# Fewer loaded bytes and an earlier buffer release in a kernel of strided sparse attention and spectral mixing on one core

## The chip, the cores and the metric

The kernel runs on one core of a Trainium2 chip. The metric is the device time of one execution in microseconds. Three executions of the kernel before gave 451.14 us as their median (450.7 to 451.53).

## The reference, cut to what matters

```python
# attention: q, k, v are (8 batches, 8 heads, 576, 64)
scores = q @ k.T / 8
mask   = local (0 <= rel < 32) for heads 0-3, strided (rel >= 0, same residue mod 32) for heads 4-7
x      = softmax(where(mask, scores, -1e9)) @ v            # -> (8, 576, 512)
# spectral mixing: w_r, w_i are (64 modes, 512, 512), w_ch is (512, 512)
X  = rfft(x, axis=1)[:, :64]
Yr = Xr @ w_r - Xi @ w_i          # per mode
Yi = Xr @ w_i + Xi @ w_r
u  = x + irfft(Y, n=576)
out = u + relu(u @ w_ch)
```

Two facts carry the change. The 128 MiB of w_r and w_i in float32 are by far the largest input. And in mode 0 of a real signal Xi is zero and the inverse transform ignores Yi, so w_i of mode 0 is never needed.

## The kernel before

The program has four stages on one instruction order per engine. First the strided heads of 8 batches (to about 99 us). Then the local heads, interleaved with the 64 modes of one half of the channels. Then the 64 modes of the other half, interleaved with transposes of x and products with w_ch. Last a tail that turns spectra into rows and writes the result.

Weights come as float32 and are written as float16 by transfers that GpSimd issues. One mode and half is a tile, filled by two transfers of 256 KB:

```python
for ri, src in enumerate([moe_w_r, moe_w_i]):       # w_fetch
    nc.gpsimd.dma_start(wt[ds(64 * ri, 64)],
        src[m, ds(256 * half, 256), :].rearrange("(p c) e -> p c e", c=4))
```

Twelve buffers and six "guest" places (modes 3 to 6, and 16 and 17, in memory that other data needs later) hold 18 tiles. `mode(slot, m)` does a mode's 16 matmuls and then asks for one more tile, unless its own tile was a guest:

```python
if slot or m not in GUEST:
    w_fetch()
```

In the second stage each batch does 8 modes, spread over 19 pieces of attention work, so mode 7 is the very last thing of batch 0:

```python
for mi in range(8):
    upto = -(-len(work) * (mi + 1) // 8)
    for w in work[n:upto]: w()
    n = upto
    mode(0, 8 * b + mi)
```

The strided stage loads q, k and v of a batch as 72 rows of 2048, three tiles deep:

```python
nc.gpsimd.dma_start(qn[0:72, vi, :],
    src[i, 4:8].rearrange("h (c r) d -> (h c) (r d)", r=32))
```

w_ch is loaded twice, once in plain order and once (`w_cp`, four transfers) in the order in which x lies. The masks are constants already repeated for three or four heads.

The softmax here doesn't subtract the row's maximum and nothing guards it: scores larger than these inputs give would overflow.

Of the kernel before, what the change touches and what calls it, by code (L numbers as in the profile page):

```python
# [11 lines left out]
F16 = mybir.dt.float16  # L12
# [6 lines left out]
DM = 512  # L19
# [10 lines left out]
def _host_consts():  # L30
    s = np.arange(S)
    m = np.arange(NM)
    ang = 2.0 * np.pi * np.outer(s, m) / S
    F3 = np.stack([np.sin(ang), np.cos(ang), -np.sin(ang)], axis=1)
    F3 = F3.reshape(S, 3 * NM)

    Fl = np.zeros((128, 5, 3 * NM))
    for t in range(5):
        Fl[: SCS[t], t] = F3[128 * t : 128 * t + SCS[t]]
    Fs = np.zeros((128, 6, 3 * NM))  # L40
    for rp in range(2):
        for j, (a, z) in enumerate(JG):
            r2 = np.arange(a, z)
            ss = (32 * np.arange(NCB)[None, :] + 2 * r2[:, None] + rp).reshape(-1)
            Fs[: len(ss), 3 * rp + j] = F3[ss]



    A = np.zeros((4, 2, 16, S))
    for mm in range(NM):  # L50
        e = np.zeros(S // 2 + 1, dtype=np.complex128)
        for ri, unit in enumerate((1.0, 1j)):
            e[mm] = unit
            A[mm // 16, ri, mm % 16] = np.fft.irfft(e, n=S)
    A = A.reshape(2 * NM, S)
    A[:, :512] = A[:, :512].reshape(128, 256, 2).transpose(0, 2, 1).reshape(128, 512)

    ms = []
    for nr in (6, 5):
        n = nr * NCB  # L60
        kc, kr = np.arange(n) // nr, np.arange(n) % nr
        qr, qc = np.arange(n) // NCB, np.arange(n) % NCB
        ok = (kr[:, None] == qr[None, :]) & (kc[:, None] <= qc[None, :])
        blk = np.zeros((128, n))
        blk[:n] = np.where(ok, 0.0, NEG)
        ms.append(np.tile(blk, (1, 4)))

    rel = np.arange(160)[None, :] - np.arange(128)[:, None]
    blk = np.where((rel >= 0) & (rel < STRIDE), 0.0, NEG)
    ma = np.tile(blk, (1, 3))  # L70
    last = np.full((128, 96), NEG)
    last[:64, 32:] = blk[:64, :64]
    mb = np.tile(np.concatenate([blk, last], axis=1), (1, 2))
    f16 = [a.astype(np.float16) for a in (Fl, Fs, A, ms[0], ms[1], ma, mb)]
    return f16 + [np.eye(128, dtype=np.float16)]


# [1 line left out]
def kernel(  # L79
# [31 lines left out]
        return pss[kind].tile([128, 512], FP, tag=kind, name=kind)  # L111

    hosts = _host_consts()
    names = ["cFl", "cFs", "cA", "cM6", "cM5", "cMa", "cMb", "cI"]
    drams = {
        n: nc.inline_tensor(np.ascontiguousarray(h), name=n).ap()
        for n, h in zip(names, hosts)
# [5 lines left out]
    def const_load(eng, *which):  # L123
        for n in which:
            eng.dma_start(cs[n], drams[n])

    idn = cs["cI"]


    XC = [0, 2, 1, 3]  # L130
# [33 lines left out]
    def w_fetch(n=1):  # L164
        for _ in range(n):
            i = len(w_tiles)
            if i >= 2 * NM:
                return
            half, m = 1 - i // NM, i % NM
            if i in GUEST:  # L170
                n, j = GUEST[i]
                if j == 0:
                    guests[n] = big.tile([128, 2, 4, DM], F16, tag=n, name="wt")
                wt = guests[n][:, j]
            else:
                wt = pw.tile([128, 4, DM], F16, tag="w", name="wt")
            for ri, src in enumerate([moe_w_r, moe_w_i]):
                nc.gpsimd.dma_start(  # L178
                    wt[ds(64 * ri, 64)],
                    src[m, ds(256 * half, 256), :].rearrange("(p c) e -> p c e", c=4),  # L180
                )
            w_tiles.append(wt)

    def w_cp_fetch():
        w_cp = pw.tile([128, 4, DM], F16, tag="w", name="w_cp")
        for c2 in range(2):
            for half in range(2):
                nc.gpsimd.dma_start(
                    w_cp[ds(64 * c2, 64), ds(2 * half, 2), :],
                    moe_w_ch[ds(256 * half, 256), :].rearrange(  # L190
                        "(p cp c2) e -> c2 p cp e", cp=2, c2=2
                    )[c2],
                )
        w_chs["cp"] = w_cp


    qns = {}
# [113 lines left out]
    def str_scores(b, t):  # L311
        qT, kz = qTs[b % 2], kzs[b % 2]
        j, rp = STR[t]
        a, z = JG[j]
        n = (z - a) * NCB
        mask = cs["cM6"] if j == 0 else cs["cM5"]
        scp = psum("sc")
        nc.tensor.matmul(scp[:, 0 : 4 * n], idn, mask, start=True, stop=False)
        for h in range(4):
            nc.tensor.matmul(  # L320
                scp[:, ds(n * h, n)],
                kz[:, rp, ds(72 * a + n * h, 128)],
                qT[:, ds(288 * h + a * NCB, n)],
                start=False,
                stop=(h == 3),
            )
        nc.scalar.activation(  # L327
            out=PS[0:n, ds(POFF[t], 4 * n)],
            in_=scp[0:n, 0 : 4 * n],
            func=ACTF.Exp,  # L330
            scale=SCALE,
        )
# [71 lines left out]
    def loc_scores(b, h, tail):  # L404
        par, hp = b % 2, h // 2
        scp = psum("sc")
        nc.tensor.matmul(  # L407
            scp if tail else scp[:, 0:480],
            idn,
            cs["cMb"] if tail else cs["cMa"],  # L410
            start=True,
            stop=False,
        )
        todo = []
        if tail:
            for hh in range(2):
                todo.append((256 * hh, 576 * hh + 384, 160))
                todo.append((256 * hh + 192, 576 * hh + 512, 64))
        else:
            for t in range(3):  # L420
                todo.append((160 * t, 576 * (h % 2) + 128 * t, 160))
        for i, (col, s0, n) in enumerate(todo):
            nc.tensor.matmul(  # L423
                scp[:, ds(col, n)],
                kzs[par][:, hp, ds(s0, 128)],
                qTs[par][:, ds(s0, n)],
                start=False,
                stop=(i == len(todo) - 1),
            )
        PV = PL[:, 0:4096].rearrange("p (h x) -> p h x", h=4)  # L430
        if tail:
            dst = PV[:, ds(2 * hp, 2), 768:1024]
            src = scp.rearrange("p (h x) -> p h x", h=2)
        else:
            dst = PV[:, h, 0:768].rearrange("p (t x) -> p t x", t=3)[:, :, 0:160]
            src = scp[:, 0:480].rearrange("p (t x) -> p t x", t=3)
        nc.scalar.activation(out=dst, in_=src, func=ACTF.Exp, scale=SCALE)  # L437
# [64 lines left out]
    def mode(slot, m):  # L502
        half = 1 - slot
        mi, mg = m % 8, m // 8
        if mi == 0:
            ypt[slot] = psum("y")
        yp = ypt[slot]
        yv = yp.rearrange("p (m e x) -> p m e x", m=8, e=4)
        wt = w_tiles[slot * NM + m]
        for e in range(4):  # L510
            for c in range(4):
                nc.tensor.matmul(  # L512
                    yv[:, mi, e, :],
                    wt[:, XC[c], ds(128 * e, 128)],
                    Xh[half][:, c, :, :, m],
                    start=(c == 0),
                    stop=(c == 3),
                )
        if slot or m not in GUEST:
            w_fetch()  # L520
        if mi == 7:
            part = (slice(None), slice(None), mg // 2, slice(None), ds(8 * (mg % 2), 8))
            src = yp.rearrange("p (m e x) -> p e x m", m=8, e=4)
            if slot == 0:
                if m == 7:
                    spectra_tile("Y0")
                nc.scalar.activation(out=YS["Y0"][part], in_=src, func=ACTF.Copy)
            else:
                nc.vector.tensor_tensor(
                    out=YS["YT"][part], in0=src, in1=YS["Y0"][part], op=AluOp.add  # L530
                )
# [134 lines left out]
    load(0)  # L666
    const_load(nc.scalar, "cI", "cM6", "cM5", "cFs")
    load(1)
    const_load(nc.sync, "cMa", "cMb", "cFl", "cA")
    load(2)  # L670
    w_fetch(2)

# [54 lines left out]


    psum_pools(tp=2, sc=2, av=2, y=2)
    for b in range(B):  # L730
        load(B + b + 3)
        front = loc_front(b + 1)
# [6 lines left out]
            values[2], front[6], values[3], front[7], lambda: dft(b, 0),  # L739
        ]  # L740
        if b == 6:
            work.insert(0, w_cp_fetch)
        n = 0
        for mi in range(8):
            upto = -(-len(work) * (mi + 1) // 8)
            for w in work[n:upto]:
                w()
            n = upto
            mode(0, 8 * b + mi)
    actx.close()  # L750
    spectra_tile("YT")

# [3 lines left out]
    xoh = [ptr.tile([128, DM], F16, name=f"xoh{i}") for i in range(4)]  # L756
    zzs = [ptr.tile([128, DM], F16, name=f"zz{i}") for i in range(B)]
    yys = [ptr.tile([128, DM], F16, name=f"yy{i}") for i in range(B)]
    w_chs["n"] = ptr.tile([128, 4, DM], F16, name="w_ch")
    nc.gpsimd.dma_start(w_chs["n"], moe_w_ch.rearrange("(c p) e -> p c e", p=128))  # L760
    work = []
    for b in range(B):
        for half, cp in ((1, 0), (1, 1), (0, 0), (0, 1)):
            work.append(lambda b=b, half=half, cp=cp: turn(b, half, cp))
# [128 lines left out]
```

## Time and profile before

| what | value | how to read it |
|---|---|---|
| span of the profiled execution | 448.4 us | the profile's own clock; the measured time is about 2 us more |
| share of software DMA queue | 94.1% of 16 engines | weights, q, k, v and w_ch |
| chain that ended last | DMA 52%, TensorE 19% | followed back from the last instruction |
| TensorE busy | 341.4 us (76%) | not the bound |
| last weight landed | 408.37 us | from the semaphore records of the trace |
| tail after it | 40.0 us | 448.4 - 408.4 |

A software transfer here ends with one completion from each of the 16 DMA engines, and the trace has the time of each. The Trainium skill, "DMA: Bandwidth & Descriptors", Why a DMA increments its semaphore by 16 and not by 1, describes it so: all 16 engines post one increment, each behind its own data. The trace agrees: every one of these transfers has 16 completion times. The completion times carry no engine's number: "the last engine" below is the one that came last for that transfer, and need not be the same one each time.

### The profile page before, as it was taken

The numbers are of one execution on the slowest core, as the hardware profiler recorded it, in microseconds if no ns is written. First come the engines' busy times: TensorE is split into PE (matmuls) and PEld (weight loads), VectorE is DVE, ScalarE is ACT, GpSimd is POOL, SyncE is SP. The second block draws the span as 40 slices with busy tenths as digits, with TensorE's granted clock in tenths as the row PEclk, the third lists the DMA queues.
The fourth block names the chain that finished last, engine by engine and source line by source line (L and its number), as shares of the span: only waits on it lengthen the run. The fifth ranks groups of instructions, "written<-read, shape, count | busy, mean of one in ns | idle before, by whom it ended". The sixth has DMA issues, their size and how long they took to land.

```text
span 448.4 us, 12268 instructions
## 1 busy us (share of the span) xinstructions
PE 341.4 (76%) x5269; PEld 242.9 (54%) x5269; DVE 215.0 (48%) x461; ACT 185.8 (41%) x349; POOL 183.1 (41%) x332
## 2 busy tenths in 40 slices
PE   2887687769898986848875585877859687787994
PEld 2766576647676865646654353545536454543441
DVE  3687767846443542323311242336344543542895
ACT  1586666554554552514341120213314221342883
POOL 4233333332544343444444343434344444420773
PEclk9998979899987895756555575768797886888999
DMA  8999999999999999999999999999999999992687
GB/s 200 197 198 200 203 197 203 209 211 208 165 211 210 214 210 212 210 213 212 212 207 208 212 212 211 212 212 211 213 203 212 213 211 212 212 211 48 261 313 272
DMA packets 31637, 93.72 MB, mean 209 GB/s; under 512 B 5792, under 2 KB 7584, under 8 KB 31584
## 3 DMA queue, kind: packets, MB, share of 16 engines
q0 software_dynamic: 27344, 82.33, 94.1%
q1 hardware_dynamic: 3664, 10.09, 6.1%
q8 instruction: 41, 0.67, 0.6%
q10 hardware_dynamic: 576, 0.53, 0.4%
q14 instruction: 12, 0.10, 0.1%
HBM read 165.80 MB, written 9.44 MB: 391 GB/s over the span
## 4 chain that ended last, share of the span: by engine, by line
DMA 52%; PE 19%; issue 3%; ACT 2%; DVE 1%; POOL 0%; DVEq 0%; ACTq 0%; POOLq 0%
DMA wt<-in_moe_w_i_dram 43%; DMA wt<-in_moe_w_r_dram 6%; PE y L512 4%; DMA qn<-in_k_dram 2%; PE tp L362 2%; PE v L803 2%; PE sc L407 2%; PE v L634 1%; PE u L652 1%; PE y L480 1%; PE sc L423 1%; PE u L650 1%; PE av L444 1%; ACT X L233 1%; PE z L621 1%
## 5 line engine op out<-in xcount | busy, mean ns | idle before, releaser
L512 PE MATMUL y<-X,wt 128*128 128x16 f16 x2048 | 83.0, 192 | 67.2 <-DMA wt<-in_moe_w_i_dram 62.1
L178 POOL DMA_DIRECT2D wt<-in_moe_w_r_dram x128 | 66.3, 518 | 122.1 <-DMA wt<-in_moe_w_r_dram 30.4
L512 PEld LDWEIGHTS <-wt 128*128 128x128 f16 x2048 | 72.8, 103 | 79.7 <-issue 71.7
L178 POOL DMA_DIRECT2D wt<-in_moe_w_i_dram x128 | 66.2, 517 | 74.3 <-DMA wt<-in_moe_w_i_dram 41.3
L608 ACT ACTIVATE v<-sc 128x512 f16<-128x512 f32 x32 | 19.1, 597 | 88.2 <-PE sc L599 88.2
L599 PE MATMUL sc<-w_cp,xT 128*128 128x512 f16 (+1 forms) x160 | 52.4, 457 | 0.5 <-DVE xT L571 0.5
L437 ACT ACTIVATE PL<-sc 128x480 f16<-128x480 f32 (+1 forms) x48 | 27.3, 579 | 50.9 <-PE sc L423 49.7
L609 DVE COPY xo<-tp 128x512 f16<-128x512 f16 x32 | 22.1, 692 | 50.7 <-PE tp L607 50.7
L223 DVE TENSOR_TENSOR xb<-av,rec 90x256 f16<-90x256 f32 (+2 forms) x80 | 36.0, 450 | 2.8
L222 DVE RECIPROCAL rec<-av 90x4 f32<-90x4 f32 (+2 forms) x80 | 14.7, 184 | 42.0 <-PE av L452 29.0
L369 DVE COPY qT<-tp 128x576 f16<-128x576 f16 x16 | 12.1, 759 | 40.8 <-PE tp L362 36.7
L233 ACT ACTIVATE v<-tp 128x640 f16<-128x640 f16 (+1 forms) x24 | 19.4, 807 | 23.2 <-PE tp L396 19.7
L362 PE MATMUL tp<-cI_s,qn 64*64 64x64 f16 x864 | 25.9, 210 | 3.4 <-DMA qn<-in_q_dram 2.2
L327 ACT ACTIVATE PS<-sc 90x360 f16<-90x360 f32 (+1 forms) x48 | 22.7, 488 | 11.0 <-PE sc L320 10.5
L827 DVE TENSOR_TENSOR osb<-u,rl 128x512 f32<-128x512 f32 x36 | 23.3, 688 | 6.2 <-ACT rl L812 3.2
L815 POOL TENSOR_TENSOR rl<-rl,xo 128x512 f32<-128x512 f32 x15 | 17.3, 1158 | 20.0 <-ACT rl L812 19.6
L362 PEld LDWEIGHTS <-qn 64*64 64x64 f16 x864 | 20.3, 123 | 9.0 <-issue 3.8
L258 PE MATMUL tp<-cI_s,qn 72*128 72x72 f16 x256 | 15.1, 209 | 12.5 <-DMA qn<-in_v_dram 9.6
L627 ACT ACTIVATE zz<-av 32x512 f16<-32x512 f32 x24 | 14.1, 588 | 24.1 <-PE av L621 23.9
L369 DVE COPY vT<-tp 128x576 f16<-128x576 f16 x16 | 12.1, 758 | 23.5 <-PE tp L362 23.5
L423 PE MATMUL sc<-qT,kz 128*128 128x160 f16 (+1 forms) x160 | 23.0, 272 | 0.0
L599 PEld LDWEIGHTS <-xT 128*128 128x128 f16 (+1 forms) x160 | 14.7, 110 | 15.3 <-issue 7.2
(91 smaller groups left out, 659.3 us busy)
## 6 DMA issues: line engine op xcount, KB each, us to landing
wt<-in_moe_w_r_dram POOLq DMA_DIRECT2D x128, 256.0 KB, 9.4
wt<-in_moe_w_i_dram POOLq DMA_DIRECT2D x128, 256.0 KB, 9.6
out_dram<-osb SPq DMA_DIRECT2D x15, 512.0 KB, 2.7
qn<-in_v_dram POOLq DMA_DIRECT2D x16, 288.0 KB, 10.5
qn<-in_q_dram POOLq DMA_DIRECT2D x16, 288.0 KB, 10.8
qn<-in_k_dram POOLq DMA_DIRECT2D x16, 288.0 KB, 10.7
out_dram<-osb SPq DMA_DIRECT2D x8, 128.0 KB, 2.4
w_cp<-in_moe_w_ch_dram POOLq DMA_DIRECT2D x4, 128.0 KB, 8.2
```

Source lines behind the costliest of these rows:

```text
L178: nc.gpsimd.dma_start(wt[ds(64 * ri, 64)], src[m, ds(256 * half, 256), :].rearrange("(p c) e -> p c e", c=4),)
L223: nc.vector.tensor_tensor(out=dst, in0=val.rearrange("p h (q c) -> p h c q", c=4), in1=rec[0:n, 0:pieces] .to_broadcast((n, pieces, 64)) . ...
L233: nc.scalar.activation(out=out, in_=in_, func=ACTF.Copy)
L327: nc.scalar.activation(out=PS[0:n, ds(POFF[t], 4 * n)], in_=scp[0:n, 0 : 4 * n], func=ACTF.Exp, scale=SCALE,)
L362: nc.tensor.transpose(tp[ds(64 * hp, 64), ds(64 * i, 64)], qn[ds(64 * hp, 64), vi, ds(64 * (9 * g + i), 64)], idn[ds(64 * hp, 64), ds(64 * ...
L369: eng(out=dst.rearrange("p (h s i) -> p h s i", h=2, i=18)[:, :, :, ds(9 * g, 9)], in_=tp[pr, 0:576].rearrange("p (i h s) -> p h s i", h=2 ...
L423: nc.tensor.matmul(scp[:, ds(col, n)], kzs[par][:, hp, ds(s0, 128)], qTs[par][:, ds(s0, n)], start=False, stop=(i == len(todo) - 1),)
L437: nc.scalar.activation(out=dst, in_=src, func=ACTF.Exp, scale=SCALE)
L512: nc.tensor.matmul(yv[:, mi, e, :], wt[:, XC[c], ds(128 * e, 128)], Xh[half][:, c, :, :, m], start=(c == 0), stop=(c == 3),)
L599: nc.tensor.matmul(vp[pr, :], xT[:, ch, cols], w_chs["cp"][:, ch, :], start=(ch == 0), stop=(ch == 3),)
L609: nc.vector.tensor_copy(out=xo[pr].rearrange("p (h q c) -> p h q c", h=2, c=4), in_=tp[pr, 0:512].rearrange("p (h c q) -> p h q c", h=2, c=4),
L827: nc.vector.tensor_tensor(out=osb[:, t % 2, :], in0=up, in1=rls[b, t][:, t % 2, :], op=AluOp.add)
```

## The change

The intent is to move fewer bytes, as the transfers bound the kernel, and to close the one visible pause of the transfers. w_ch is read once and reordered on chip; w_i of mode 0 is left out; masks are stored for one head and repeated by the access pattern; the early batches do more modes.

```diff
-        ms.append(np.tile(blk, (1, 4)))
+        ms.append(blk)
...
+    def mask_rows(name, n, times):
+        return cs[name][:, 0:n].unsqueeze(1).broadcast_to((128, times, n))
...
-            for ri, src in enumerate([moe_w_r, moe_w_i]):
+            for ri, src in enumerate([moe_w_r, moe_w_i] if m else [moe_w_r]):
...
-    def w_cp_fetch():            # four transfers of 128 KB, w_ch in another order
+    def w_ch_fetch():            # the one load of w_ch, at the place of the other
...
+        pr = ds(0, 128 if m else 64)      # mode 0: 64 of the 128 rows
...
+    NMODES = [11, 9, 8, 8, 7, 7, 7, 7]
...
-        for mi in range(8):
-            upto = -(-len(work) * (mi + 1) // 8)
+        nm = NMODES[b]
+        for mi in range(nm):
+            upto = -(-len(work) * (mi + 1) // nm)
...
+    def w_turn(half, cp):        # 4 of these, before the third stage's other work
+        wp = psum("sc")
+        for c2 in range(2):
+            for i in range(2):
+                a = 64 * c2 + 32 * i
+                nc.tensor.matmul(wp[ds(a, 32), :],
+                    idn.rearrange("p (x c) -> p c x", c=4)[:, 2 * cp + c2, :],
+                    w_chs["n"][:, 2 * half + i, :],
+                    start=True, stop=True, tile_position=(0, a))
+        act_copy(w_chs["cp"][:, 2 * half + cp, :], wp)
```

More of the change, by code (lines that the diff above doesn't have):

```diff
@@ L65, in _host_consts @@
         blk[:n] = np.where(ok, 0.0, NEG)
-        ms.append(np.tile(blk, (1, 4)))
+        ms.append(blk)
     rel = np.arange(160)[None, :] - np.arange(128)[:, None]
     blk = np.where((rel >= 0) & (rel < STRIDE), 0.0, NEG)
-    ma = np.tile(blk, (1, 3))
     last = np.full((128, 96), NEG)
     last[:64, 32:] = blk[:64, :64]
-    mb = np.tile(np.concatenate([blk, last], axis=1), (1, 2))
-    f16 = [a.astype(np.float16) for a in (Fl, Fs, A, ms[0], ms[1], ma, mb)]
+    ml = np.concatenate([blk, last], axis=1)
+    f16 = [a.astype(np.float16) for a in (Fl, Fs, A, ms[0], ms[1], ml)]
     return f16 + [np.eye(128, dtype=np.float16)]
@@ L113 @@
     hosts = _host_consts()
-    names = ["cFl", "cFs", "cA", "cM6", "cM5", "cMa", "cMb", "cI"]
+    names = ["cFl", "cFs", "cA", "cM6", "cM5", "cMl", "cI"]
     drams = {
@@ L182, in w_fetch @@
             w_tiles.append(wt)
-    def w_cp_fetch():
-        w_cp = pw.tile([128, 4, DM], F16, tag="w", name="w_cp")
-        for c2 in range(2):
-            for half in range(2):
-                nc.gpsimd.dma_start(
-                    w_cp[ds(64 * c2, 64), ds(2 * half, 2), :],
-                    moe_w_ch[ds(256 * half, 256), :].rearrange(
-                        "(p cp c2) e -> c2 p cp e", cp=2, c2=2
-                    )[c2],
-                )
-        w_chs["cp"] = w_cp
+    def w_ch_fetch():
+        w_ch = pw.tile([128, 4, DM], F16, tag="w", name="w_ch")
+        nc.gpsimd.dma_start(w_ch, moe_w_ch.rearrange("(c p) e -> p c e", p=128))
+        w_chs["n"] = w_ch
     qns = {}
@@ L315, in str_scores @@
         n = (z - a) * NCB
-        mask = cs["cM6"] if j == 0 else cs["cM5"]
+        mask = mask_rows("cM6" if j == 0 else "cM5", n, 4)
         scp = psum("sc")
-        nc.tensor.matmul(scp[:, 0 : 4 * n], idn, mask, start=True, stop=False)
+        nc.tensor.matmul(
+            scp[:, 0 : 4 * n].rearrange("p (h x) -> p h x", h=4),
+            idn,
+            mask,
+            start=True,
+            stop=False,
+        )
         for h in range(4):
@@ L406, in loc_scores @@
         scp = psum("sc")
+        n, times = (256, 2) if tail else (160, 3)
         nc.tensor.matmul(
-            scp if tail else scp[:, 0:480],
+            scp[:, 0 : n * times].rearrange("p (h x) -> p h x", h=times),
             idn,
-            cs["cMb"] if tail else cs["cMa"],
+            mask_rows("cMl", n, times),
             start=True,
@@ L513, in mode @@
                     yv[:, mi, e, :],
-                    wt[:, XC[c], ds(128 * e, 128)],
-                    Xh[half][:, c, :, :, m],
+                    wt[pr, XC[c], ds(128 * e, 128)],
+                    Xh[half][pr, c, :, :, m],
                     start=(c == 0),
@@ L668 @@
     load(1)
-    const_load(nc.sync, "cMa", "cMb", "cFl", "cA")
+    const_load(nc.sync, "cMl", "cFl", "cA")
     load(2)
@@ L741 @@
         if b == 6:
-            work.insert(0, w_cp_fetch)
+            work.insert(0, w_ch_fetch)
         n = 0
-        for mi in range(8):
-            upto = -(-len(work) * (mi + 1) // 8)
+        nm = NMODES[b]
+        for mi in range(nm):
+            upto = -(-len(work) * (mi + 1) // nm)
             for w in work[n:upto]:
@@ L748 @@
             n = upto
-            mode(0, 8 * b + mi)
+            mode(0, sum(NMODES[:b]) + mi)
     actx.close()
@@ L758 @@
     yys = [ptr.tile([128, DM], F16, name=f"yy{i}") for i in range(B)]
-    w_chs["n"] = ptr.tile([128, 4, DM], F16, name="w_ch")
-    nc.gpsimd.dma_start(w_chs["n"], moe_w_ch.rearrange("(c p) e -> p c e", p=128))
-    work = []
+    w_chs["cp"] = ptr.tile([128, 4, DM], F16, name="w_cp")
+    def w_turn(half, cp):
[3 more added lines that the diff above has]
+                a = 64 * c2 + 32 * i
+                nc.tensor.matmul(
+                    wp[ds(a, 32), :],
+                    idn.rearrange("p (x c) -> p c x", c=4)[:, 2 * cp + c2, :],
+                    w_chs["n"][:, 2 * half + i, :],
+                    start=True,
+                    stop=True,
+                    tile_position=(0, a),
+                )
+        act_copy(w_chs["cp"][:, 2 * half + cp, :], wp)
+    work = [
+        lambda half=half, cp=cp: w_turn(half, cp) for half in range(2) for cp in range(2)
+    ]
     for b in range(B):
```

## The prediction

> **What bounds the kernel now.** I read four views in this order: the 40 slices of the page, the chain that ended last, the busy time of each stretch, and the timeline of GpSimd, which issues nearly all loads.
>
> ```profile
> DMA  8999999999999999999999999999999999992687
> GB/s 200 197 198 200 203 197 203 209 211 208 165 211 210 214 210 212 210 213 212 212 207 208 212 212 211 212 212 211 213 203 212 213 211 212 212 211 48 261 313 272
> q0 software_dynamic: 27344, 82.33, 94.1%
> DMA 52%; PE 19%; issue 3%; ACT 2%; DVE 1%; POOL 0%; DVEq 0%; ACTq 0%; POOLq 0%
> wt<-in_moe_w_r_dram POOLq DMA_DIRECT2D x128, 256.0 KB, 9.4
> ```
>
> The 16 DMA engines are 90% busy or more from the first slices to slice 36 (408 us). Only one slice sags, the eleventh, 165 GB/s where its neighbours have 208 and 211. The chain is DMA for 52% of the span, nearly all of it weight loads between 162 and 408 us. From 408.4 us, when the last weight has landed, to 448.4 us there follows a tail of TensorE, ScalarE and VectorE that the diff hardly touches. So the time is (when the last weight lands) + about 40 us, and the first term is the bytes of one queue at its rate, plus the gaps.
>
> The gap, in single microseconds (length; busy time and count of PE, PEld, DVE, ACT, POOL; PE clock; DMA share; GB/s), and what the issuing engine did (start, duration, what, idle before it and its releaser):
>
> ```profile
> 111.00:112.00 1.00, 0.94 (x18) 0.63 (x14) 0.50 (x2) 0.68 (x2) 0.00 (x0) 1.00 1.07 213
> 112.00:113.00 1.00, 1.00 (x14) 0.63 (x13) 0.00 (x0) 0.33 (x2) 0.00 (x0) 1.00 0.89 180
> 113.00:114.00 1.00, 1.00 (x30) 0.76 (x28) 0.00 (x0) 0.98 (x3) 0.23 (x1) 1.00 0.48 94
> 114.00:115.00 1.00, 1.00 (x36) 0.85 (x31) 0.67 (x1) 0.96 (x3) 1.00 (x3) 1.00 0.33 57
> 115.00:116.00 1.00, 0.62 (x14) 0.41 (x10) 0.09 (x1) 1.00 (x3) 1.00 (x3) 1.00 1.14 152
> ```
>
> ```profile
> 107.41 0.52 POOL L178 DMA_DIRECT2D wt<-in_moe_w_i_dram  x1 [0.65 <-DMA qn<-in_v_dram]
> 113.78 0.52 POOL L178 DMA_DIRECT2D wt<-in_moe_w_r_dram  x1 [5.85 <-PE y L512]
> 114.28 0.52 POOL L178 DMA_DIRECT2D wt<-in_moe_w_i_dram  x1
> ```
>
> GpSimd waits 5.85 us for a mode's matmuls. Eighteen weight tiles are prefetched when the second phase begins at about 99 us; modes 0, 1 and 2 each free a buffer and are refetched, modes 3 to 6 sit in guest tiles and free nothing, and mode 7 stands at the very end of batch 0, behind all its attention work. The transfers in flight run out at about 112.6 us. In 110 to 120 us the core moved 1.61 MB where 212 GB/s would have given 2.12 MB (742 KB and 868 KB in its two halves, from the packet records): 0.5 MB, or 2.3 us.
>
> In the first phase (15 to 98 us) the stretch view shows 202 GB/s and a DMA share of 1.05, and TensorE waits for the loads of q and v: 2.0 and 0.2 us in 45 to 60, and in 75 to 90:
>
> ```profile
> PE tp L362 <- DMA qn<-in_q_dram: 2.2, 1, 2.2
> PE tp L242 <- DMA qn<-in_q_dram: 1.1, 1, 1.1
> ```
>
> So this phase too is paced by the transfers, with some 6 us of slack in TensorE's own work.
>
> **What the Trainium skill says.** "DMA: Bandwidth & Descriptors", Rules for kernel authors, says of two transfers to disjoint partition halves that they "serialize", because both spray over all 16 engines. This matters: w_r goes to partitions 0-63 and w_i to 64-127, and if each half had its own eight engines, leaving out w_i alone would gain nothing. The trace agrees with the page: in the steady part, completions of w_r and w_i alternate evenly, 1.24 us apart (197.38, 198.62, 199.87, 201.10 us for their first), on all 16 engines. One left-out half is therefore 1.24 us. The same page, Why small descriptors are slow, speaks of a fixed overhead per packet. The packet records agree: a 4096-byte packet took 324 ns (79 ns per KB), a 1024-byte packet, which is what both loads of w_ch consist of, 98 ns, 24% more per byte. "HBM Reference", Specifications, puts about 358 GB/s to a core when both of a pair stream, and says that one alone gets well above it; here 391 GB/s are read and written over the whole span, so the 16 engines' packets and not the memory's share are what I count.
>
> **The change, part by part.**
> - Second load of w_ch (w_cp): four DMAs of 128 KB disappear. 512 packets of 98 ns over 16 engines is 3.1 us of busy time; at the usual share of 1.06 that is 2.9 us. The landing times say the same: the four follow one another at 0.65 us (2.6 us), and the next DMAs are some 0.3 us late. It lies in the DMA-bound stretch (230 us): **-2.9 us**. The other load of w_ch stays, only moved earlier into that place. It costs what it cost.
> - In its place: 16 matmuls of 512 columns and four ScalarE copies. By the kernel's own 512-column matmuls with w_cp (380 ns median) and copies (597 ns) that is 6 us of TensorE and 2.4 us of ScalarE at the start of the last mode phase, where TensorE is busy 4.5 to 6.4 of every 10 us and ScalarE 1 to 3. It delays no transfer: the weights are four modes in flight, and TensorE may fall several modes behind before a buffer is missing. 0 us.
> - w_i of mode 0, left out in both halves: 1.24 us in the last mode phase, certain (**-1.2 us**); and once in the first phase, where at 202 GB/s it is **-1.3 us** if the phase follows.
> - Masks: packets of 864, 720, 960 and 1024 bytes, 128 of each, took 0.32 + 0.35 + 0.57 + 0.39 = 1.63 us of the 16 engines' time. In their place come 216, 180 and 512 bytes; the identity's 256-byte packets took 18 ns, 0.14 us per constant, so about 0.5 us in all: **-1.1 us**, in the first 10 us, where the first load of v (awaited until 6.9 us) stands beside them. TensorE reads the same number of mask columns, so I take the repeated read as free.
> - More modes first: batch 0 gets 11 instead of 8, and mode 7 comes after 14 of the 19 attention pieces, not after all. In the old trace the 14th ends at 108.5 us; with two more modes ahead of it (0.5 us each) mode 7 ends at about 110, before the old gap. Everything is about 2.4 us earlier (masks and first w_i), so it ends at about 107.6 us while transfers in flight would last to 110.2; data flowed 1.5 us after the issue in the old gap. The gap closes with half a microsecond to spare: **-2.3 us**. Modes 8, 9, 10 follow closely, so no new gap; the guests 16 and 17 in batch 1 leave a pause of three modes (5 us) against some 10 us in flight.
>
> Sum: 2.9 + 1.2 + 1.3 + 1.1 + 2.3 = 8.8 us, of which 4.1 are as good as certain and 4.7 depend on the first phase. I take off 0.3 for the closing of the gap, which is tight, and predict 451.14 - 8.5 = 442.6 us.
>
> **The rivals.** (1) *The first phase follows its compute, not its transfers.* Between 15 and 45 us no TensorE wait for DMA is seen, and VectorE is busy some 8 of 10 us. Then the 2.4 us saved early only make transfers run dry sooner, at the same buffer limit: the gap would start 2.4 us earlier than mode 7 can. For it: the cap of 18 tiles. Against it: the waits of 6 us for q and v. It would leave 4.1 + about 2.3, so 444.8 us. (2) *The gap only moves*, because of the guests or because the larger batch 0 delays the next batches' loads: 4.1 + 2.4, also 444.6 us. (3) *The eight slow engines.* At the end of the stream half of the engines finish 3 us before the others (405.2 against 408.4 us). Were the unfinished half loaded by something the change does not remove, the gain would shrink; but all removed transfers touch all 16. (4) *TensorE's slow clock*: it was granted 0.5 at 410 to 412 us, right after the wait for the last weight, and the first matmuls of the tail took double. If it falls otherwise, the tail moves by 1 us either way.
>
> **Range and chances.** All gains point one way, and nothing is added to the path that I can find, so slower is all but excluded. The low end is everything, with w_cp at 3.2 us, and a luckier clock in the tail: 440.5. The high end is the certain part and little of the rest: 445.6. The 2% line is at 442.1 us, only half a microsecond under my number. I put 0.4 on the faster side, as the first-phase terms can only fall short.
>
> **What would show each step right or wrong.** GB/s of the eleventh slice at 205 or more, and GpSimd's wait before mode 7's refetch under 2 us (gap); second phase beginning some 2 us earlier, and TensorE's waits for q and v no longer than before (first phase); spacing of weight completions still 1.24 us and last landing at about 400 us; HBM reads down by some 2.4 MB from 165.8; the tail still 40 us. Wrong would be: a new sag, a second phase that begins at 99 us as before, or a longer tail because w_ch now holds one of the twelve buffers that the output tiles share until its middle.

## The result

The changed kernel took 444.51 us (median of 4, 443.73 to 445.32), against 450.92 us of the kernel before in the same rounds. The ratio is 0.9857, with a 95% interval of 0.9832 to 0.9881: faster by 1.4%. All ratios here are the mean time of one kernel's runs over that of the other's of the same rounds, so not quite the ratio of the medians beside them. The time lies inside the predicted range (440.5 to 445.6); the gain of 6.4 us is 2.1 us short of the predicted 8.5.

The page after, the lines that answer to those of before (slices, queue, chain):

```profile
DMA  8999999999999999999999999999999999991687
GB/s 187 179 204 203 201 197 207 209 212 208 205 212 212 212 212 210 210 212 212 212 209 212 212 212 211 212 212 211 210 195 211 213 211 213 213 207 23 263 321 275
q0 software_dynamic: 26608, 81.28, 94.0%
HBM read 163.37 MB, written 9.44 MB: 391 GB/s over the span
DMA 57%; PE 15%; issue 3%; ACT 1%; DVEq 0%; DVE 0%; ACTq 0%; POOLq 0%
```

The eleventh slice now stands at 205 GB/s instead of 165: the pause is gone. The bytes are gone too: 2.43 MB fewer are read (165.80 to 163.37). In single microseconds and on GpSimd (columns as in the prediction):

```profile
109.00:110.00 1.00, 0.99 (x30) 0.87 (x27) 0.88 (x3) 0.61 (x2) 0.48 (x1) 1.00 1.03 205
110.00:111.00 1.00, 1.00 (x37) 1.00 (x33) 0.53 (x3) 0.73 (x2) 0.87 (x3) 1.00 1.10 205
111.00:112.00 1.00, 0.96 (x19) 0.68 (x15) 0.41 (x1) 0.67 (x1) 0.98 (x3) 1.00 0.96 168
112.00:113.00 1.00, 1.00 (x16) 0.66 (x16) 0.00 (x0) 0.18 (x1) 0.76 (x2) 1.00 1.06 209
```

```profile
104.13 0.52 POOL L181 DMA_DIRECT2D wt<-in_moe_w_i_dram  x1
109.52 0.52 POOL L181 DMA_DIRECT2D wt<-in_moe_w_r_dram  x1 [4.87 <-PE av L455]
110.02 0.52 POOL L181 DMA_DIRECT2D wt<-in_moe_w_i_dram  x1
```

GpSimd still waits 4.87 us for mode 7, but now it is released at 109.5 us, before the transfers in flight have run out. (The view names the matmul of another tile, av, as the releaser; mode 7's own matmuls ended at 109.2 us by the timeline of TensorE.) So all four parts did what they were meant to do. The last weight landed at 401.90 us instead of 408.37, which is the whole 6.5 us; the tail is 40.0 us in both profiles.

Where, then, are the other 2 us? I lined up the transfers of the two profiles by name and compared when the **last of the 16 engines** completed each. This is not a view of the profile but worked out from its semaphore records, for the w_r half of each tile (the last row is the last transfer of all, a w_i half):

```
weight tile          before    after    ahead by   (tiles 0-63: one half, 64-127: the other)
3                     36.1      33.7      2.4      early savings are in
17 (before the gap)  104.5     101.3      3.2
29 (after the gap)   143.3     139.7      3.7      the gap gave 0.4, not 2.3
58 (before w_ch)     229.7     226.1      3.6
80 (after w_ch)      289.6     282.4      7.2      w_ch and half of w_i of mode 0
120                  389.8     382.6      7.2
last of all          408.4     401.9      6.5
```

Before the gap the last engine is ahead by what the prediction expected, and more (3.2 for 2.4; part of it comes from one late completion at 99.65 us in the profile of before). Closing the gap added only 0.4 us. The 16 completions around it, in the kernel before, say why (#77 was issued before GpSimd's wait, #78 after it):

```
       issued    first of 16   median   last of 16
#76    106.24      111.54      112.49     116.12
#77    107.41      112.78      113.72     117.39
#78    113.78      117.02      117.28     118.64
#79    114.28      118.27      118.54     119.86
```

The last engine completes at steps of 1.25 us across the gap, as everywhere. The median engine makes a step of 3.56 us there: it ran dry. One engine was nearly 2 us behind the next one; while the others stood still, it worked off its backlog, and the stream ends when the last engine ends. The mean over 16 engines, from which I took 0.5 MB and 2.3 us, cannot show this. This is the reading of one pair of profiles; the table of all profiles below tests it.

### The profile page after: what moved, and what is told of

It reads as the page before. It is cut to its first block, busy times and chain, and to the rows that moved or that the text cites. A ratio compares the mean times of both kernels' runs of the same rounds, so it can differ in the third digit from the quotient of the medians.

```text
span 441.9 us, 12293 instructions
## 1 busy us (share of the span) xinstructions
PE 342.7 (78%) x5285; PEld 243.2 (55%) x5285; DVE 214.8 (49%) x461; ACT 188.0 (43%) x353; POOL 179.6 (41%) x326
## 3 DMA queue, kind: packets, MB, share of 16 engines
HBM read 163.37 MB, written 9.44 MB: 391 GB/s over the span
## 4 chain that ended last, share of the span: by engine, by line
DMA 57%; PE 15%; issue 3%; ACT 1%; DVEq 0%; DVE 0%; ACTq 0%; POOLq 0%
DMA wt<-in_moe_w_i_dram 46%; DMA wt<-in_moe_w_r_dram 9%; PE y L516 3%; DMA qn<-in_k_dram 2%; PE v L827 2%; PE tp L364 2%; PE v L638 1%; PE u L656 1%; PE sc L410 1%; PE sc L426 1%; PE u L654 1%; PE y L483 1%; PE av L447 1%; PE z L625 1%; PE tp L398 0%
## 5 line engine op out<-in xcount | busy, mean ns | idle before, releaser
L516 PE MATMUL y<-X,wt 128*128 128x16 f16 (+1 forms) x2048 | 83.0, 192 | 62.7 <-DMA wt<-in_moe_w_i_dram 58.8
L516 PEld LDWEIGHTS <-wt 128*128 128x128 f16 (+1 forms) x2048 | 72.9, 103 | 75.6 <-issue 50.4
L181 POOL DMA_DIRECT2D wt<-in_moe_w_i_dram x126 | 65.1, 517 | 62.6 <-DMA wt<-in_moe_w_i_dram 38.6
L603 PE MATMUL sc<-w_cp,xT 128*128 128x512 f16 (+1 forms) x160 | 54.4, 471 | 0.9 <-DVE xT L575 0.9
L483 PEld LDWEIGHTS <-xb 108*128 108x128 f16 (+2 forms) x176 | 17.9, 118 | 11.9 <-DVE xb L219 6.2
L603 PEld LDWEIGHTS <-xT 128*128 128x128 f16 (+1 forms) x160 | 15.0, 112 | 16.7 <-issue 8.6
L410 PE MATMUL sc<-cMl_s,cI_s 128*128 128x480 f16 (+1 forms) x48 | 22.0, 459 | 1.6 <-ACT X L229 1.6
L611 PEld LDWEIGHTS <-xT 128*128 128x128 f16 (+1 forms) x160 | 15.2, 117 | 13.5 <-issue 7.2
```

Source lines behind the costliest of these rows:

```text
L181: nc.gpsimd.dma_start(wt[ds(64 * ri, 64)], src[m, ds(256 * half, 256), :].rearrange("(p c) e -> p c e", c=4),)
L410: nc.tensor.matmul(scp[:, 0 : n * times].rearrange("p (h x) -> p h x", h=times), idn, mask_rows("cMl", n, times), start=True, stop=False,)
L483: nc.tensor.matmul(xp[:, ds(192 * cp, 192)], xb[b][0:n, base + t, ds(128 * cp, 128)], F[0:n, t, :], start=(i == 0), stop=(i == len(tiles) ...
L516: nc.tensor.matmul(yv[:, mi, e, :], wt[pr, XC[c], ds(128 * e, 128)], Xh[half][pr, c, :, :, m], start=(c == 0), stop=(c == 3),)
L603: nc.tensor.matmul(vp[pr, :], xT[:, ch, cols], w_chs["cp"][:, ch, :], start=(ch == 0), stop=(ch == 3),)
```

## The experiments

**Theory S**, formed from the above: the slowest engine sets the stream's end, and the gap was mostly time in which other engines waited. **Theory M**, the rival and my prediction: the mean share counts. From the first runs a third reading grew, **theory L**: the wait for mode 7 is a limit that stays put when the transfers get faster early on, so early savings alone are lost there, and the new numbers of modes are what keeps them. One us is 0.0022 of a ratio.

| run | median us | before, same rounds | ratio (95%) |
|---|---|---|---|
| n1_modes_only | 449.97 | 450.81 | 0.9968 (0.9943 to 0.9994) |
| m1_masks_only | 450.62 | 450.81 | 0.9983 (0.9956 to 1.0009) |
| w1_wch_only | 447.70 | 450.81 | 0.9929 (0.9900 to 0.9959) |
| i1_wi0_only | 450.07 | 450.81 | 0.9990 (0.9952 to 1.0029) |
| a1_after_8each | 447.02 | 451.46 | 0.9900 (0.9870 to 0.9930) |
| d1_mode7_late | 453.98 | 451.46 | 1.0043 (1.0010 to 1.0076) |
| q1_rows_64_8 | 443.00 | 451.46 | 0.9806 (0.9778 to 0.9834) |
| e1_early_and_modes | 448.68 | 451.33 | 0.9939 (0.9920 to 0.9957) |
| q2_before_rows_64_8 | 451.93 | 451.33 | 1.0009 (0.9974 to 1.0043) |
| q3_rows_more_modes | 443.80 | 451.33 | 0.9840 (0.9817 to 0.9863) |
| s0_eight_rows_side0 | 450.12 | 450.73 | 0.9995 (0.9975 to 1.0015) |
| s1_eight_rows_side1 | 449.82 | 450.73 | 0.9992 (0.9967 to 1.0016) |

d2 did not build (below). All of these gave the right result, and all are "same" by the 2% line but q1, which is unclear as its interval lies across the line. For each profiled execution I also read the step between the two transfers around mode 7's wait, for the last and the median of the 16 engines (an undisturbed step is 1.24 us), and how far the last engine was ahead of the profile of the kernel before at tile 17 (before the wait) and at tile 58 (well after it):

```
                   issue after the wait   last engine   median engine   ahead at 17   at 58
before                   113.78              1.25           3.56             0          0
n1_modes_only            111.53              1.26           1.58            0.6        0.5
m1_masks_only            112.27              1.24           3.23            2.5        2.0
w1_wch_only              115.47              1.22           3.38           -1.5       -1.5
i1_wi0_only              118.34              5.34           6.76            1.2       -3.9
a1_after_8each           111.98              1.61           2.88            3.0        2.4
d1_mode7_late            120.70              2.42           5.28           -0.3       -2.8
q2_before_rows_64_8      115.19              4.43           4.85            3.6       -0.6
e1_early_and_modes       109.02              1.23           1.21            3.3        3.4
after                    109.52              1.24           1.23            3.2        3.6
q1_rows_64_8             108.30              1.22           1.43            5.3        6.2
q3_rows_more_modes       109.52              3.02           2.11            5.6        4.8
s0_eight_rows_side0      113.13              1.08           1.22            0.3        0.5
s1_eight_rows_side1      112.98              1.24           1.23           -1.0       -0.5
```

Two things can be read here. Where only the median engine's step was long (m1, w1, a1), the last engine kept its lead within 0.6 us; where the last engine's step was long too (i1, d1, q2), it lost 2.5 to 5.1 us of it and did not get them back (in q3, with its step 1.8 us too long, 0.8). So within one execution it is the last engine that counts. But mode 7 came anywhere from 108 to 121 us, so one profile does not say what its kernel loses as a rule: those of m1 and a1 are the fastest of their six executions, those of i1 and w1 the slowest.

### One part at a time

**n1**: the kernel before with the new numbers of modes.

```diff
+    NMODES = [11, 9, 8, 8, 7, 7, 7, 7]     # on the kernel before, as in the change
```

> The kernel before with 11, 9, 8, 8, 7, 7, 7, 7 modes in the batches and nothing else changed. Theory S (the stream ends when the slowest of the 16 engines ends, and the sag at 113 us was time in which 15 engines were dry while the slowest still worked off its backlog): gain of 0 to 0.6 us, 450.3 to 450.9, though the profile shows the sag gone. Theory M, that of my prediction (the mean share of the engines counts): gain 2.3 us, 448.6.

Measured: 0.8 us by the medians, 1.4 by the ratio. That lies between the 2.3 of theory M and the 0 to 0.6 of theory S, and the interval (0.3 to 2.6 us) excludes neither. In the profile the gap is closed (0.92 as the lowest DMA share of a microsecond between 110 and 118 us, where the kernel before has 0.33), and its last weight landed at 408.01 us, only 0.36 before the other's. So in this profile closing the gap was worth next to nothing, but on average it is not free: the slowest engine's reserve differs between executions, as i1 shows.

**m1**: the small masks alone; **i1**: w_i of mode 0 left out, alone.

```diff
-        ms.append(np.tile(blk, (1, 4)))                          # m1, with its uses
+        ms.append(blk)
```
```diff
-            for ri, src in enumerate([moe_w_r, moe_w_i]):        # i1, with 64-row matmuls
+            for ri, src in enumerate([moe_w_r, moe_w_i] if m else [moe_w_r]):
```

> The kernel before with the small masks alone. Theory S and my prediction agree on the size if the first phase follows its transfers: 1.1 us less engine time early. But with 8 modes in batch 0 the transfers run dry 1 us sooner; under S the slowest engine has some 2 us to spare there, so the 1.1 us are kept (449.8); under M they are lost at the buffer limit (450.9, no gain).

> The kernel before without the imaginary weights of mode 0, nothing else. S: 1.24 us in each phase, 2.5 us less (448.4), as the slowest engine does its share of both halves and the early saving is kept. M: the early half is lost at the buffer limit, 1.2 us less (449.7).

m1 gained 0.2 us by the medians (0.8 by the ratio), i1 0.7 (0.5 by the ratio), and neither interval excludes zero. m1 settles nothing: its interval, from 0.4 us slower to 2.0 faster, holds both S's 1.1 and M's 0, and its own profile kept most of the early lead. i1 speaks for M's 1.2 us, as its interval (1.3 slower to 2.2 faster) just excludes S's 2.5; but not even the late half (1.24 us) comes out clearly, and the six times spread from 448.96 to 454.22 us. The profiled execution of i1 is the slowest of the six and shows how the limit can bite (stretches, with the TensorE clock as the third number from the end):

```profile
100.00:105.00 5.00, 4.01 (x49) 2.46 (x50) 0.76 (x1) 2.06 (x5) 0.61 (x2) 0.50 1.03 198
105.00:110.00 5.00, 5.00 (x120) 4.42 (x120) 2.98 (x6) 1.89 (x3) 2.50 (x5) 0.50 1.00 180
110.00:115.00 5.00, 5.00 (x107) 3.80 (x105) 2.53 (x6) 1.90 (x4) 0.00 (x0) 0.63 0.93 170
115.00:120.00 5.00, 4.68 (x99) 3.54 (x97) 1.60 (x4) 3.88 (x9) 1.66 (x4) 1.00 0.14 18
```

TensorE was granted half its clock just when batch 0 ran, and mode 7 came at 118 us instead of 114 (2.2 us of this because the second phase had begun that much later). This time the slowest engine ran dry as well: its step was 5.34 us, 4.1 more than an undisturbed one. The gap's cost is thus a matter of how late mode 7 is and how far behind the last engine lags: nothing in one profile, 4 us in another. No run changed the clock alone, so its part in this is argued.

**w1**: w_ch read once and reordered by TensorE, alone.

```diff
-            work.insert(0, w_cp_fetch)      # and the later load of w_ch dropped
+            work.insert(0, w_ch_fetch)      # and w_turn, as in the change
```

> The kernel before with the channel weights read once and reordered by TensorE, nothing else. Both theories: 2.5 to 2.9 us less (448.0 to 448.4). The first figure is what the landing times of the two profiles give (lead 3.5 us before both loads, 7.2 after, less 1.24 for the left-out half), the second the predicted one. A rival, that the reordering delays the start of the last mode phase, would make it under 2 us.

3.1 us less by the medians, 3.2 by the ratio: the predicted 2.9 holds. This saving lies behind mode 7, whose wait therefore cannot take it away. The profiled execution was the slowest of the six (450.73); there the lead grew by 2.1 us from tile 58 to tile 80. The reordering in the changed kernel:

```profile
L773 PE MATMUL sc<-w_ch,cI_s x16: 611/613/634, 245.2 to 249.7; 128*32 128x512 f16 x16
```

The matmuls took 613 ns (median), not the 380 that the prediction borrowed from another line, as TensorE had its slow clock there. It made no difference that can be seen: the slice from 243 to 254 us still moved 212 GB/s, and w1 gained what was predicted.

### The modes on top of the other parts, and later instead of earlier

**a1**: the changed kernel with 8 modes in each batch. **d1**: the kernel before with mode 7 later. **d2**: later still.

```diff
-    NMODES = [11, 9, 8, 8, 7, 7, 7, 7]
+    NMODES = [8, 8, 8, 8, 8, 8, 8, 8]        # a1
+    NMODES = [6, 8, 9, 9, 8, 8, 8, 8]        # d1, on the kernel before
+    NMODES = [6, 4, 10, 10, 9, 9, 8, 8]      # d2, on the kernel before
```

> The changed kernel with 8 modes in every batch again. Theory S: the slowest engine is 2.4 us further ahead than in the kernel before when mode 7 frees its buffer, about as much as it had to spare, so 0 to 1 us slower than the changed kernel (444.5 to 445.5). Theory M: the whole sag comes back and the 2.4 us saved early are lost too, 447 to 449.

> The kernel before with 6, 8, 9, 9, 8, 8, 8, 8 modes, so that mode 7, whose buffer the transfers wait for, comes some 2 us later than in the kernel before. Theory S: the slowest engine had 2.3 us to spare, so 0 to 0.5 us slower (451 to 451.5). Theory M: 2 us slower (453).

> The kernel before with 6, 4, 10, 10, 9, 9, 8, 8 modes, so that mode 7 comes some 5 us later. Theory S: 2 to 3 us slower, as the slowest engine now runs dry as well (453 to 454). Theory M: 5 us slower (456).

a1 took 447.02 us, in the range of theory M (447 to 449) and not of S (444.5 to 445.5). It gained 4.4 us over the kernel before, against 6.4 of the whole change: on top of the other parts the modes are worth some 2 us, more than the 0.8 to 1.4 that they gain alone. The two were not timed in the same rounds, and their intervals (3.2 to 5.9 and 5.4 to 7.6 us) just overlap. In d1 the delay of mode 7 cost 2.5 us by the medians (1.9 by the ratio), the 2 us of theory M and not the 0 to 0.5 of theory S: the reserve of 2.3 us that I had read from one profile was not there in most executions. Its profile has mode 7 released 6.9 us later, but d1 also issues q, k and v of the next batch before it (4.0 us of transfers), which leaves 2.9; the slowest engine's step was 1.2 us too long. d2: in that order the transfers and the modes wait for each other (a deadlock), and it did not run.

**e1**: the kernel before with everything early, that is masks, mode 0 without w_i in the first half only, and the new numbers of modes.

```diff
+            for ri, src in enumerate([moe_w_r, moe_w_i] if i else [moe_w_r]):   # first tile only
+    NMODES = [11, 9, 8, 8, 7, 7, 7, 7]                                          # and the masks of m1
```

> The kernel before with the small masks, mode 0 without imaginary weights in the first half only, and the new numbers of modes: all that my prediction counted as early, 2.4 us saved and the gap of 2.3 us closed. My prediction: 4.4 us less (446.5). Theory L (early savings alone are lost at the buffer limit, the modes alone gain under 1 us because the slowest engine hardly ran dry, and only together are the early savings kept): about 2 us less, 448.5 to 449.3, which is what the whole change leaves after the runs with one part.

2.65 us less (interval 1.9 to 3.6), for which the prediction had 4.4 (2.4 saved early, 2.3 of gap, 0.3 taken off). This run excludes the prediction's sum. It does not say which of the two terms was too large: 2.65 is the early saving and next to nothing for the gap, or, as in a1, some 2 us for the gap and little for early savings that would be lost without it. Of the forecasts of theory S so far, n1 and m1 leave it undecided and i1, a1 and d1 went against it. What stays of it is that the last engine's break is the one that costs time; its reserve, read from one profile, is not the same in every execution.

### Is it the heaviest engine?

The completions of the 72-row loads show two engines some 4 to 7 us ahead of the other 14. The Trainium skill, "DMA: Bandwidth & Descriptors", Why a DMA increments its semaphore by 16 and not by 1, tells of an exception on trn2 in which some copies put the rounded-up sixteenth of the partitions on each engine. For 72 rows that would be five on 14 engines, two on one and none on the last, and the trace agrees with two light engines. 64 rows would be four on each.

**q1** (on the changed kernel) and **q2** (on the kernel before):

```diff
-                nc.gpsimd.dma_start(qn[0:72, vi, :], rows)
+                nc.gpsimd.dma_start(qn[0:64, vi, :], rows[0:64])
+                nc.gpsimd.dma_start(qn[64:72, vi, :], rows[64:72])
```

> The changed kernel with each 72-row load of q, k and v split into one of 64 rows and one of 8. In the profile two of the 16 engines finish every 72-row load some 7 us before the others, as if 14 engines carried five rows each and the other two next to none; 64 rows are four for each, and the 8 left take turns. If the heaviest engine counts (S), it carries half a row less per load: 24 loads of half a packet of 327 ns, up to 3.9 us less in the first phase, of which TensorE's waits for q and v allow about 2 (442.5). If the mean counts (M): no gain, or a loss of 0.5 us for 24 more loads in the queue of eight (444.5 to 445).

> The kernel before with the 72-row loads split into 64 and 8 rows. Theory L: the heaviest engine saves about 2 us in the first phase as on the changed kernel, but with 8 modes in batch 0 nearly all of it is lost at the buffer limit: 0 to 0.8 us less (450 to 450.8). A rival, that the split gains something later than the limit, would keep the 1.5 us that it gave on the changed kernel (449.3).

q1 took 443.00 us (442.41 to 443.72), and its ratio of 0.9806 stands beside 0.9857 for the changed kernel: some 1.5 to 2.3 us more, though the two were not timed in the same rounds. The bytes are the same. The distance between first and last completion of a transfer fell from 6.8 to 2.1 us (means of 30 to 40 us), and the last weight landed at 399.26 us, 2.6 earlier. The tail after it was 41.9 us instead of 40.0, so this execution kept only 0.8 us of that; TensorE had half its clock for some 6 us of it, in the changed kernel's for some 3. So an even load on the engines is worth time at equal bytes, as theory S expected (442.5). It is also the fastest of all kernels here.

On the kernel before the same edit gained nothing (451.93 against 451.33; the interval, 1.2 us faster to 1.9 slower, excludes the 1.5 that it gave on the changed kernel). Its six times fall into two groups, 449.8 to 450.7 and 453.1 to 454.5, and the profile is of the slower one. In the profile of q2 the weights of mode 17 landed at 100.9 us, 3.6 ahead of the kernel before, and then:

```profile
112.00:113.00 1.00, 0.96 (x28) 0.79 (x25) 0.69 (x2) 0.66 (x2) 0.00 (x0) 1.00 1.03 205
113.00:114.00 1.00, 1.00 (x9) 0.63 (x9) 0.00 (x0) 0.69 (x1) 0.00 (x0) 1.00 0.44 90
114.00:115.00 1.00, 1.00 (x21) 0.77 (x20) 0.00 (x0) 0.66 (x2) 0.00 (x0) 1.00 0.02 4
115.00:116.00 1.00, 1.00 (x26) 0.72 (x25) 0.25 (x1) 0.95 (x4) 0.81 (x2) 1.00 0.00 0
116.00:117.00 1.00, 0.65 (x20) 0.56 (x18) 0.51 (x1) 1.00 (x3) 1.00 (x3) 1.00 0.70 66
```

All 16 engines stand still for some two microseconds (DMA share 0.02 and 0.00, the second number from the end) where the kernel before kept at least 0.33. The slowest engine's step is 4.43 us, 3.2 more than undisturbed: the early lead is handed back at the limit. Together with a1 this is theory L: an early saving counts for sure only if mode 7 comes early enough.

**q3**: still more modes in front, on top of q1.

```diff
+    NMODES = [13, 11, 9, 8, 6, 6, 6, 5]
```

> The changed kernel with the split loads and 13, 11, 9, 8, 6, 6, 6, 5 modes. In the profile of the split alone the slowest engine's landings were not interrupted at mode 7 (steps of 1.22 us), so theory S sees nothing left to gain: 443.0 within 0.5. If the median engine counted, its shorter wait would give about 1 us more (442).

443.80 us, ratio 0.9840: no gain over q1, if anything a loss of 0.8 us. It was to test whether earlier releases are worth nothing once the slowest engine passes mode 7 without a break, but its profile does not show that case. There the second phase began at 99.1 us instead of q1's 96.4, mode 7 was released at 109.5 instead of 108.3, and the slowest engine's step was 3.02 us. So the question stays open.

**s0 and s1**: an attempt to use the engines' order at the end (on q1's kernel, 18 of the 24 eight-row rests are steered to one group of eight engines in s0 and to the other in s1, if small transfers take turns between two groups). At the end of the stream half of the engines finish earlier, in the changed kernel by up to 4.2 us (397.7 to 401.9), in the kernel before by 3.2, in the other profiles by 3.3 to 4.9. The end of the changed kernel's stream:

```profile
397.00:398.00 1.00, 1.00 (x21) 0.99 (x19) 0.34 (x1) 0.60 (x1) 0.00 (x0) 0.50 0.73 143
398.00:399.00 1.00, 1.00 (x8) 0.51 (x5) 0.35 (x1) 0.00 (x0) 0.00 (x0) 0.77 0.49 98
399.00:400.00 1.00, 0.99 (x22) 0.75 (x20) 0.46 (x1) 0.59 (x1) 0.00 (x0) 1.00 0.39 78
400.00:401.00 1.00, 0.15 (x5) 0.03 (x1) 0.23 (x1) 0.00 (x0) 0.00 (x0) 1.00 0.15 29
401.00:402.00 1.00, 0.00 (x0) 0.00 (x0) 0.00 (x0) 0.00 (x0) 0.00 (x0) 0.94 0.02 4
```

In the last microsecond hardly anything moves, and everything waits for it. 16 KB instruction fetches of about 0.95 us each, 42 in the whole profile, are a candidate for what loads some engines more; no run tests it.

```diff
+                if turn8[0] != want:      # a small transfer turns the order of the groups
+                    nc.gpsimd.dma_start(qn[64:72, vi, 0:16], rows[64:72, 0:16])
+                    nc.gpsimd.dma_start(qn[64:72, vi, 16:], rows[64:72, 16:])
```

> The changed kernel with the 72-row loads split, and the 8-row rests placed by small extra transfers so that 18 of the 24 fall on one group of eight engines and 6 on the other, if such transfers take turns between two groups. In the profiles eight engines finish some 4 us after the other eight, and 16 KB instruction fetches of 0.95 us, five for each of eight engines if they take turns, would make that difference. If so, 6 packets of 327 ns moved from the late group to the early one end the stream up to 2 us sooner for one side (441 to 442.5), and up to 2 us later for the other (444 to 445). If the placement has no effect or the late group is not fixed, both are at 443.0 within 0.5.

> As the run before, with the other group of eight engines carrying 18 of the 24 rests: the opposite sign of it is expected against 443.0 us if the late eight engines are a fixed group, the same 443.0 within 0.5 if they are not.

Both failed, 450.12 and 449.82 us, 7 us slower than q1 and with no difference between them. The first stage became slower with the 13 (s0) and 12 (s1) extra small transfers: it moved 182 to 196 GB/s between 20 and 80 us, where q1 moved 200 to 211, and mode 17 landed at 104.2 and 105.5 us instead of 99.2. (TensorE's clock was lower as well, 0.83 to 0.89 from 40 to 80 us where q1 had 1.00; which came first is not shown.) A small transfer takes one of the eight places in flight (each one waits for the one issued eight before it). Whether the late engines are a fixed group, and what loads them, stays open.

## Why the prediction was right or wrong

The number was 1.9 us low (442.6 for 444.5), the range and the side of the line held. The 4.1 us that it called as good as certain make up most of the 6.4. The sums that it gave for rivals 1 and 2 (444.8 and 444.6) lie nearer to the result than its own. For rival 2 that is luck, as no new sag appeared after the eleventh slice. By its own steps:

- **What bounds the kernel**: right. The end moved by what the last landing moved, and the tail stayed at 40.0 us. That is not so in every execution: in the other profiles the tail took 40.2 to 43.9 us, where rival 4 had allowed for 1 us.
- **w_ch, 2.9 us**: right; 3.1 measured alone.
- **w_i of mode 0, late half, 1.2 us**: consistent with the lead of the last engine (3.6 to 7.2 us over both late parts, 3.6 for predicted 4.1), but the run that isolates it, i1, was too scattered to show it.
- **Masks and w_i early, 2.4 us, through a first phase paced by its transfers**: right in the whole change. The last engine was 2.4 us ahead at tile 3, the second phase began at 99.1 instead of 101.1 us, and TensorE's waits for q and v shrank:

```profile
PE tp L364 <- DMA qn<-in_q_dram: 1.8, 1, 1.8
```

  That is 1.8 us in 75 to 90 us where 3.3 stood before.
- **The gap, "0.5 MB, or 2.3 us"**: too large beside the early savings. This is the term that failed: 2.4 and 2.3 were to give 4.4 together and gave 2.65 (e1). The gap alone measured 0.4 us in the two profiles and 0.8 to 1.4 when closed alone; on top of the other parts it was some 2 us (the change against a1). In the profiles of before and after, the bytes missing from the mean were missing on engines that had time to spare; the one that ends last had no pause. Even the mean says less than 2.3 when it is read as busy time: the stretch view has a DMA share of 0.90 in 110 to 120 us and 1.07 in 120 to 160, which is about 1.6 us. The skill's "Perfetto Trace Analysis", What "DMA-bound" means, lists "Specific DMA engines" as the first of three things that can bind, and I did not take it up. The table of steps agrees: in m1 the median engine's step was 2.0 us too long and the last engine's not at all.
- **Adding the terms up**: wrong in form. They are not independent. By the medians, masks alone and the split rows alone gained 0.2 and -0.6 us, the modes alone 0.8, everything early together 2.65. Rival 1 described the limit that eats early savings; a1 and q2 bear it out on average, m1 leaves it open, and the fourth part of the change is what disarms it.
- **Mode 7 at 107.6 us, GpSimd's wait under 2 us**: late by 1.6 us (mode 7 ended at 109.2, issue at 109.5, wait 4.87). TensorE had half its clock from 95 to 101 us, in the kernel before only from 99 to 102, which is a likely cause. It was early enough.
- **Rival 3, the slow engines**: dismissed because all removed transfers touch all 16. That holds for transfers, not for a pause. At the end the distance between first and last engine grew from 3.2 to 4.2 us, and the lead of the last engine fell from 7.2 to 6.5; but m1, w1 and d1 also show 3.9 to 4.2, so this need not come from the change.
- **Small slips in the working**: 98 ns for 1024 bytes against 324 for 4096 is 21% more per byte, not 24%. In 110 to 120 us the stretch view gives 164 GB/s, so 1.64 MB and not 1.61; the 2.3 us stay. Rival 1's sum is 444.7. None of them changes the argument.

Parts measured apart, 2.65 (e1) + 3.1 (w1) + 1.2 (late half, estimated from the landing step) make 7.0 us; the whole measured 6.4. The 0.6 is within what executions of one kernel differ by, and I cannot assign it.

## What to carry to other kernels

A dip in the mean DMA rate need not be a loss of that size: look at the last of the 16 completions of each transfer, and count only the break in that one, in more than one profile. A saving ahead of a full buffer can be lost unless the buffer is also released earlier, so test parts of a change together as well as alone. Where a load's rows do not divide evenly over the 16 engines, splitting off the uneven rest can gain time at the same bytes, but every extra transfer costs a place in the queue.

## What the Trainium skill lacked or had wrong

- "Perfetto Trace Analysis", What "DMA-bound" means, names specific engines as a bound and points to a track for each, but does not say that a pause can be read from the completions: here the mean lost 0.5 MB (2.3 us) in a pause that cost the stream 0.4 us in one pair of profiles, and the 16 completion times of each transfer showed it.
- "DMA: Bandwidth & Descriptors", Why a DMA increments its semaphore by 16 and not by 1, gives its exception for 100 and 127 partitions. For 72 rows two engines completed some 4 to 7 us before the others, and 64 + 8 rows brought the spread from 6.8 to 2.1 us and the time from 444.5 to 443.0 us.
- The same page ties casting to GpSimd but gives no rate for it: a packet that writes 4096 bytes of float16 from float32 took 324 ns, one of 4096 bytes without a cast (the output) 160 ns, and the stream held 212 GB/s written, 1.24 us per 256 KB. As the first reads 8192 bytes, both move about 25 bytes per ns on their wider side: here the float32 bytes set the time, and no cost of the cast itself is seen.
- No page of it that I read says that a slow clock of TensorE may hold up a DMA-bound stream, through the release of buffers: in i1, at half clock from 100 to 110 us, mode 7 came 4.6 us later (2.2 of them from a later start) and the slowest engine lost 4.1 us. No run isolates the clock.
